# Overlapping the first two local-attention chunks, cutting TensorE work into shorter pieces, and a new set of plan constants, in a two-layer attention kernel

## The chip, the cores and the metric

One core of one Trainium2 chip runs the whole program. The metric is the device time of one execution in microseconds (us). The profile shows five engines, each with its own list of instructions: TensorE (PE in the profile; PEld is its weight loads), VectorE (DVE), ScalarE (ACT), GpSimd (POOL) and SyncE (SP).

## The reference, cut to what matters

```python
x = A_x                                                  # 1 x 2048 x 512, bf16
x = x + _A_ref(_layernorm(x), A_wqkv, A_wo)              # local attention
x = x + _B_ref(_layernorm(x), B_wq, B_wk, B_wv, B_wo)    # global attention
x = x + _A_ref(_layernorm(x), A_wqkv, A_wo)              # and both again,
x = x + _B_ref(_layernorm(x), B_wq, B_wk, B_wv, B_wo)    # with the same weights

# _A_ref: 32 heads of 16; position s sees s, s-2, ..., s-14 (8 keys, those below 0 masked)
# _B_ref: 32 query heads of 16, one shared key and value head, all 2048 keys, no mask
```

The global attention is the bulk: 32 heads x 2048 queries x 2048 keys, twice. The kernel cuts it into 4096 **tiles** of 128 keys x 512 queries. The local attention is done in **chunks** of 512 positions, four for each layer; a chunk's normalisation, projections, local attention and output come first, then the Q, K and V that the global attention of the layer needs from it.

## The kernel before: the parts that matter here

The kernel is a planner. While the program is built, each piece of work is an `Op` with the engines that may do it, the duration that the planner assumes, the pieces it depends on and a priority. The planner lays the pieces on the engines, and the order that comes out is the order in each engine's list. The stream of global tiles is a `Stream`, with biases in place of priorities. A smaller key goes first:

```python
MM, SWITCH, DMA = 216.0, 101.0, 620.0
...
class Sched:
    def cands(self, e):
        for op in self.open[e]:
            s = max(op.ready, self.free_at(op.want) if op.want else 0.0)
            ...
                yield (s + op.prio - 0.1 * (s - op.ready), s, op.ready, self.issue, (e, op))
        for src in self.sources:
            yield from src.cands(e)
...
class Stream:
    BIAS = {"act": 0.0, "act2": 150.0, "vec": 180.0, "pv": 200.0, "copy": 0.0, "pass": 140.0}
```

A global tile is a score matmul group and then an exponential. ScalarE takes two tiles at a time (`st` to `pt`); VectorE takes one (`dv`) through a 16-bit integer approximation, whose first pass on four tiles (`t` to `i`) also runs on VectorE and whose second runs on GpSimd. Then TensorE multiplies with V into `o`. So two engines share the exponentials, and the planner chooses which tile goes where.

A chunk's projections are pieces of four matmuls, its value matmuls pieces of 16:

```python
    def mm_full(self, pairs, deps, name, after=0.0):
        def emit(op):
            ps = self.psum(op, [128, 512], name=name)
            for n, (lhsT, rhs) in enumerate(pairs):
                self.chain("pe", self.nc.tensor.matmul(ps[:], lhsT=lhsT, rhs=rhs, start=(n == 0),
                                                       stop=(n == len(pairs) - 1)))
        return self.op("pe", len(pairs) * MM, emit, deps, want=("bank", "aux"), solid=True, prio=self.PRIO, after=after)

    def ln(self, src, deps, after=(0.0,) * 4, quick=False):
        ...                                              # statistics of four row tiles, on VectorE
            self.chain("dve", nc.vector.tensor_scalar_add(out=ve, in0=mv[:, :, 1], scalar1=EPS))
        ag = sm.used(self.op("dve", 560.0, aggr, st, prio=self.PRIO))
        pw = ...                                         # ve ** -0.5 on GpSimd
        nm = ...                                         # -mean * rstd on VectorE
```

A local **unit** is 128 of the 512 columns and half a chunk. It has two score groups; each gets its exponential (ScalarE), its mask (VectorE) and its multiplication with V and with ones for the denominators, together in one piece on TensorE. The tiles `q`, `k`, `v`, `xnT` and `oncA` of the local attention exist once, so a chunk's projections wait until the chunk before has let go of them.

Of the kernel before, what the change touches and what calls it, by code (L numbers as in the profile page):

```python
# [427 lines left out]
MM, SWITCH, DMA = 216.0, 101.0, 620.0  # L428
LAT = {"pe": 264.0, "act": 180.0, "dve": 142.0, "pool": 120.0, "sp": 2400.0}
POOL_COL = 1.75  # L430
FAR = float("inf")
# [10 lines left out]
class Op:  # L442

    def __init__(self, engs, emit, deps=(), want=None, frees=(), prio=0.0, mode="full", sub=0, then=None, after=0.0,
                 solid=False, port=()):
        self.engs, self.emit, self.deps, self.want, self.frees = engs, emit, list(deps), want, list(frees)
        self.prio, self.mode, self.sub, self.then, self.after = prio, mode, sub, then, after
        self.solid, self.port = solid, port
        self.end = self.eng = self.buf = None
        self.left, self.waiters = 0, []  # L450
# [5 lines left out]
class Sched:  # L456
# [12 lines left out]
    def add(self, op):  # L469
        op.left = 0  # L470
        for d in op.deps:
# [7 lines left out]
    def opened(self, op):  # L479
        op.ready = max([op.after] + [d.out() for d in op.deps])  # L480
# [31 lines left out]
    def pe_run(self, mode, sub, s, t=MM, solid=False):  # L512
# [4 lines left out]
        if solid:  # L517
            self.now["pe"] = max(s, s + t - MM) + 4
# [10 lines left out]
    def cands(self, e):  # L529
        for op in self.open[e]:  # L530
# [4 lines left out]
            if s < FAR:  # L535
                yield (s + op.prio - 0.1 * (s - op.ready), s, op.ready, self.issue, (e, op))
# [3 lines left out]
    def issue(self, s, what):  # L540
# [3 lines left out]
        if op.want:  # L544
            op.buf = self.take(op.want)
        t = op.engs[e]
# [7 lines left out]
        for h in op.frees:  # L554
            self.give(h.want, h.buf, op.out())
# [25 lines left out]
class Stream:  # L581

    GROUP = 4
    BIAS = {"act": 0.0, "act2": 150.0, "vec": 180.0, "pv": 200.0, "copy": 0.0, "pass": 140.0}
# [29 lines left out]

    def cands(self, e):
        S, B = self.s, self.BIAS
        if e == "pe":
            ok = self.next_ready()
            if ok < FAR:
                tl = self.tiles[self.pos]  # L620
                s = S.pe_start("row", tl[2], max(ok, S.free_at(("slot", "exp"))))
                if s < FAR:
                    yield (s + B["act2" if self.exps else "act"], s, 0.0, self.fill_slot, None)
                s = S.pe_start("row", tl[2], max(ok, S.free_at(("bank", "vec"))))
                if s < FAR:
                    yield (s + B["vec"], s, 0.0, self.fill_vec, None)
            if self.seg < len(self.segs):
                free = S.free_at(("bank", "o")) if self.bank is None else 0.0
                if free < FAR:
                    for n, (ok, tl, src) in enumerate(self.pvs[self.seg][:24]):  # L630
                        s = S.pe_start("col", tl[2], max(ok, free))
                        yield (s + B["pv"] + n * 0.01, s, 0.0, self.pv, n)
# [229 lines left out]

class Net:

    PRIO = 0.0

    def __init__(self, ctx, tc, w, S, nlayers, out_view):
# [33 lines left out]
        self.P = Ring([tile_(f"P{n}", [128, 2, UC], BF16) for n in range(4)])  # L901
# [5 lines left out]
        nc.gpsimd.memset(self.v.t[:, :, :, :, DH:2 * DH], 0.0)  # L907
# [6 lines left out]
        self.sched = Sched({"slot": 2, "bank": 4, **res}, {"bank": ((("vec", "aux"), 3), (("vec",), 2))})  # L914
        self.blocks = [(t, a) for t in range(4) for a in range(2)]
# [10 lines left out]
        self.xo, self.onb, self.ready, self.sums = {}, {}, {}, {}  # L926

# [59 lines left out]
    def mm_full(self, pairs, deps, name, after=0.0):  # L987

        def emit(op):
            ps = self.psum(op, [128, 512], name=name)  # L990
            for n, (lhsT, rhs) in enumerate(pairs):
                self.chain("pe", self.nc.tensor.matmul(ps[:], lhsT=lhsT, rhs=rhs, start=(n == 0),  # L992
                                                       stop=(n == len(pairs) - 1)))

        return self.op("pe", len(pairs) * MM, emit, deps, want=("bank", "aux"), solid=True, prio=self.PRIO, after=after)

    def ln(self, src, deps, after=(0.0,) * 4, quick=False):
# [5 lines left out]
        for i in range(4):  # L1003
# [3 lines left out]
            st.append(sm.used(self.op("dve", 596.0, emit, [*deps[i], *sm.prev], prio=self.PRIO, after=after[i])))  # L1007

        def aggr(op):
            for i in range(4):  # L1010
                self.chain("dve", nc.vector.bn_aggr(out=mv[:, i, :], in_=stats[:, i, :]))
            self.chain("dve", nc.vector.tensor_scalar_add(out=ve, in0=mv[:, :, 1], scalar1=EPS))

        ag = sm.used(self.op("dve", 560.0, aggr, st, prio=self.PRIO))
        pw = sm.used(self.op("pool", 1150.0, lambda op: self.chain("pool", nc.gpsimd.tensor_tensor(
            out=rstd, in0=ve, in1=self.w.nhalf[:], op=ALU.pow)), [ag], prio=self.PRIO))
# [640 lines left out]
```

## Time and profile before

| | before |
|---|---|
| median of 3 runs | 1650.68 us (1649.2 to 1652.32) |
| span of the profiled run | 1647.3 us |
| granted TensorE clock, mean | 0.933 |
| VectorE: work, idle | 1444.9, 202.4 us |
| ScalarE: work, idle | 1433.7, 213.6 us |
| tiles on ScalarE, on VectorE | 2618, 1478 |

Idle is the span less the busy time. The page of the kernel before gives the busy time of every engine, and for each group of instructions the count, the busy us, the mean ns of one, and the idle time of its engine just before it with what ended it:

```profile
PE 1542.2 (94%) x16661; PEld 522.3 (32%) x16661; DVE 1444.9 (88%) x2458; ACT 1433.7 (87%) x1751; POOL 906.0 (55%) x697
...
L1290 ACT ACTIVATE pt<-st 128x1024 bf16<-128x1024 f32 x1309 | 1223.0, 1091 | 87.9 <-PE st L1275 36.8
...
L1294 DVE TENSOR_SCALAR t<-dv 128x512 int16<-128x512 f32 x1478 | 926.4, 680 | 104.2 <-PE dv L1275 103.0
...
L1173 DVE TENSOR_TENSOR P<-P,bandmask 128x288 int32<-128x288 int32 x128 | 76.2, 632 | 7.1 <-ACT P L1167 6.2
```

TensorE is the busiest by this count, but its busy time holds waits within runs. What the second and third row say is plainer: the two engines that do the exponentials stood idle 87.9 and 104.2 us just in front of them. The waits of ScalarE say on whom (us in total, times, longest):

```profile
ACT pt L1290 <- PE st L1275: 36.8, 33, 3.7
ACT pt L1290 <- PE o L1315: 34.1, 21, 9.9
ACT xn L1026 <- DVE sm L1017: 20.8, 8, 10.6
ACT logs L1211 <- PE oa L1194: 19.6, 18, 3.9
...
ACT P L1167 <- PE st L1161: 11.6, 10, 2.8
```

All are TensorE, or the chain of the normalisation (`sm`): a score bank not yet filled (`st`), a buffer not yet multiplied away (`o`), a local unit's denominators not yet there (`logs`).

### The profile page before, as it was taken

The numbers are of one execution on the slowest core, as the hardware profiler recorded it, in microseconds if no ns is written. First come the engines' busy times: TensorE is split into PE (matmuls) and PEld (weight loads), VectorE is DVE, ScalarE is ACT, GpSimd is POOL, SyncE is SP. The second block draws the span as 40 slices with busy tenths as digits, with TensorE's granted clock in tenths as the row PEclk, the third lists the DMA queues.
The fourth block names the chain that finished last, engine by engine and source line by source line (L and its number), as shares of the span: only waits on it lengthen the run. The fifth ranks groups of instructions, "written<-read, shape, count | busy, mean of one in ns | idle before, by whom it ended". The sixth has DMA issues, their size and how long they took to land.

```text
span 1647.3 us, 41270 instructions
## 1 busy us (share of the span) xinstructions
PE 1542.2 (94%) x16661; PEld 522.3 (32%) x16661; DVE 1444.9 (88%) x2458; ACT 1433.7 (87%) x1751; POOL 906.0 (55%) x697
## 2 busy tenths in 40 slices
PE   5898999998999999999989999999999999999996
PEld 3443434322432234222332224322322222222221
DVE  5587777898699987999789996989999999999995
ACT  4677777896799978999889998899999999999993
POOL 5345443555456645566455654555666656665664
PEclk9879797999799997999989998899999999999998
DMA  4011111010110011000100001000100000000000
GB/s 130 15 15 26 15 27 16 14 35 22 25 16 13 12 21 25 18 12 18 31 11 22 12 12 27 15 4 16 42 12 12 12 25 15 12 12 28 15 12 15
DMA packets 92686, 34.45 MB, mean 21 GB/s; under 512 B 80264, under 2 KB 86024, under 8 KB 92488
## 3 DMA queue, kind: packets, MB, share of 16 engines
q1 hardware_dynamic: 91624, 29.91, 8.5%
q8 instruction: 132, 2.16, 0.5%
q10 hardware_dynamic: 864, 1.84, 0.3%
q14 instruction: 66, 0.54, 0.1%
HBM read 13.53 MB, written 2.61 MB: 10 GB/s over the span
## 4 chain that ended last, share of the span: by engine, by line
PE 42%; DVE 30%; ACT 17%; issue 8%; POOL 2%; DMA 0%; DVEq 0%; ACTq 0%; POOLq 0%
DVE t L1294 21%; ACT pt L1290 16%; PE o L1315 14%; PE st L1275 9%; PE dv L1275 3%; PE y L992 3%; DVE i L1303 3%; PE q L992 2%; PE k L992 2%; PE v L1112 2%; PE oa L1194 2%; PE oa L1186 2%; PE qb L992 2%; PE st L1161 1%; DVE P L1173 1%
## 5 line engine op out<-in xcount | busy, mean ns | idle before, releaser
L1290 ACT ACTIVATE pt<-st 128x1024 bf16<-128x1024 f32 x1309 | 1223.0, 1091 | 87.9 <-PE st L1275 36.8
L1299 POOL TENSOR_TENSOR i<-t,off 128x1024 int32<-128x1024 int32 x370 | 699.2, 1890 | 583.3 <-DVE i L1303 340.5
L1294 DVE TENSOR_SCALAR t<-dv 128x512 int16<-128x512 f32 x1478 | 926.4, 680 | 104.2 <-PE dv L1275 103.0
L1315 PE MATMUL o<-i,VEd 128*32 128x512 f16 x1472 | 275.8, 408 | 4.9 <-POOL i L1299 2.5
L1315 PE MATMUL o<-i,region 128*32 128x512 f16 x1484 | 273.2, 389 | 3.2 <-POOL i L1299 2.2
L1275 PE MATMUL st<-QT,KAB 32*128 32x512 bf16 x1312 | 259.1, 402 | 14.9 <-ACT pt L1290 12.1
L1275 PE MATMUL dv<-QT,KAB 32*128 32x512 bf16 x736 | 257.9, 400 | 11.3 <-DVE t L1294 10.1
L1303 DVE TENSOR_SCALAR i<-t 128x2048 int16<-128x2048 int16 x370 | 258.0, 698 | 8.3
L1275 PE MATMUL st<-QT,region 32*128 32x512 bf16 x1306 | 253.8, 386 | 11.8 <-ACT pt L1290 9.1
L1275 PE MATMUL dv<-QT,region 32*128 32x512 bf16 x742 | 256.0, 384 | 5.4 <-DVE t L1294 4.0
L1315 PE MATMUL o<-pt,region 128*32 128x512 bf16 x1306 | 254.2, 391 | 0.0
L1315 PE MATMUL o<-pt,VEa 128*32 128x512 bf16 x1312 | 250.3, 410 | 1.6 <-DVE X L1332 0.9
L1315 PE MATMUL o<-t,region 128*32 128x512 f16 x742 | 191.5, 390 | 0.6 <-DVE t L1294 0.6
L1315 PE MATMUL o<-t,VEd 128*32 128x512 f16 x736 | 189.2, 414 | 0.0
L1275 PEld LDWEIGHTS <-KAB 32*128 32x128 bf16 x2048 | 87.8, 92 | 261.3 <-issue 255.4
L1275 PEld LDWEIGHTS <-region 32*128 32x128 bf16 x2048 | 86.6, 91 | 256.3 <-issue 251.4
L1315 PEld LDWEIGHTS <-region 128*32 128x32 f16 (+1 forms) x3532 | 79.1, 94 | 191.3 <-issue 186.7
L1315 PEld LDWEIGHTS <-VEd 128*32 128x32 f16 x2208 | 77.7, 96 | 129.1 <-issue 121.2
L1167 ACT ACTIVATE P<-st 128x576 bf16<-128x576 f32 (+1 forms) x128 | 78.8, 652 | 12.7 <-PE st L1161 11.6
L1222 POOL TENSOR_TENSOR logs<-logs 128x256 f32<-128x256 f32 x64 | 43.3, 676 | 71.8 <-ACT rec L1213 71.7
L1173 DVE TENSOR_TENSOR P<-P,bandmask 128x288 int32<-128x288 int32 x128 | 76.2, 632 | 7.1 <-ACT P L1167 6.2
L1315 PEld LDWEIGHTS <-VEa 128*32 128x32 bf16 x1312 | 57.7, 96 | 74.7 <-issue 70.6
(136 smaller groups left out, 1166.0 us busy)
## 6 DMA issues: line engine op xcount, KB each, us to landing
lb<-rd SPq DMA_DIRECT2D x31, 256.0 KB
X<-X SPq DMA_DIRECT2D x124, 32.0 KB
k<-oncA SPq DMA_DIRECT2D x56, 64.0 KB
w_sb<-in_A_wqkv_dram ACTq DMA_DIRECT2D x4, 384.0 KB
region<-in_A_x_dram SPq DMA_DIRECT2D x3, 512.0 KB
out_dram<-w_sb SPq DMA_DIRECT2D x3, 512.0 KB
S<-X SPq DMA_DIRECT2D x62, 8.0 KB
rd<-R SPq DMA_DIRECT2D x62, 8.0 KB
```

Of the source, the lines that this page charges most:

```text
L992: self.chain("pe", self.nc.tensor.matmul(ps[:], lhsT=lhsT, rhs=rhs, start=(n == 0), stop=(n == len(pairs) - 1)))
L1112: self.chain("pe", nc.tensor.matmul(ps[64 * a:64 * a + 64, i], lhsT=self.xnT.t[:, kt, kb * 64:(kb + 1) * 64], rhs=wv[:, kt, a, :, :], star ...
L1167: ex = self.op("act", act_ns(2 * ncol), lambda op, P=P, sc=sc: self.chain("act", nc.scalar.activation(out=P.t[:, :, c0:UC], in_=self.st.po ...
L1173: self.chain(op.eng, self.pick(op).tensor_tensor(out=x, in0=x, in1=self.w.band[:].unsqueeze(1).to_broadcast([128, 8, NQ // 2]), op=ALU.bit ...
L1186: self.chain("pe", nc.tensor.matmul(o[32 * r:32 * r + 32, 0, q0:q0 + w], lhsT=vv[64 * a:64 * a + 64, j, 16 * gh:16 * gh + 32], rhs=P.t[64 ...
L1222: self.chain("pool", nc.gpsimd.tensor_tensor(out=lg.t[:], in0=lg.t[:], in1=lg.t[:], op=ALU.mult))
L1275: self.chain("pe", self.nc.tensor.matmul(out, lhsT=self.KAB[l][32 * g:32 * g + 32, a, kt * 128:(kt + 1) * 128], rhs=self.QT[32 * g:32 * g ...
L1290: self.chain("act", self.nc.scalar.activation(out=self.pt[pt][:, 0:n, :], in_=self.st.pop(key)[:, 0:n, :], func=AF.Exp, scale=E_SCALE))
L1294: self.chain("dve", self.nc.vector.tensor_scalar(out=self.t[buf][:, r, :].bitcast(I16), in0=self.dv[bank][:], scalar1=-U_BIAS, scalar2=U_B ...
L1299: i = self.nc.gpsimd.tensor_tensor(out=self.i[out][:, 0:n, :].bitcast(I32), in0=self.t[buf][:, 0:n, :].bitcast(I32), in1=self.w.off2[:, 0: ...
L1303: i = self.nc.vector.tensor_scalar(out=self.i[out][:, 0:n, :].bitcast(I16), in0=self.t[buf][:, 0:n, :].bitcast(I16), scalar1=J_OFF[j], sca ...
L1315: self.chain("pe", self.nc.tensor.matmul(self.o[bank][32 * g:32 * g + 32, :], lhsT=lhsT, rhs=rhs, start=first, stop=last, tile_position=(0 ...
```

## The change

Four edits of structure and a new set of constants came together:

1. **Overlap.** The first layer's second chunk gets its own set of tiles, lent from places that are not used yet (an unused half of QT, four X accumulators, `lb`, part of KAB, one pass buffer). It no longer waits for the first chunk's.
2. **Shorter pieces.** A projection is two pieces of two matmuls, a value piece is eight matmuls, and a unit's multiplication with V is two pieces, its denominators a third. The planner may put a tile between them.
3. **Masks and normalisation.** One mask of 576 columns in place of two of 288; the add and the multiplication of the normalisation's scalars move from VectorE to GpSimd.
4. **Constants.** Every priority has a new value, so have the biases; two new rules hold back TensorE work that would delay a due tile, and let PV matmuls gather. The durations that the planner assumes changed too (a local score group 170 ns, before 300), and so did the moment from which it plans on after such a TensorE piece.

```diff
-MM, SWITCH, DMA = 216.0, 101.0, 620.0
+MM, SWITCH, DMA = 216.0, 96.0, 620.0
+AGE = 0.054
+SLACK, PATIENCE = 575.3, 176.5
...
+        due = min((src.due() for src in self.sources), default=FAR) if e == "pe" else FAR
...
-                yield (s + op.prio - 0.1 * (s - op.ready), s, op.ready, self.issue, (e, op))
+                key = s + op.prio - AGE * (s - op.ready)
+                if s + op.engs[e] + SWITCH > due + SLACK and s - op.ready < PATIENCE:
+                    key = max(key, due + 1.0)
+                yield (key, s, op.ready, self.issue, (e, op))
...
-    BIAS = {"act": 0.0, "act2": 150.0, "vec": 180.0, "pv": 200.0, "copy": 0.0, "pass": 140.0}
+    BIAS = {"act": -17.5, "act2": 659.7, "vec": 264.7, "pv": 140.5, "pv_in": 210.7, "batch": 14, "few": 9.7,
+            "copy": 15.3, "pass": 430.3}
...
-        return self.op("pe", len(pairs) * MM, emit, deps, want=("bank", "aux"), solid=True, prio=self.PRIO, after=after)
+        a = self.op("pe", half * MM, emit, deps, want=("bank", "aux"), solid=True, prio=410.8 + self.PRIO)
+        b = self.op("pe", half * MM, rest, behind=[a], solid=True, prio=-2800.5 + self.PRIO)
+        b.want, b.lend = None, a
+        return b
...
-        ag = sm.used(self.op("dve", 560.0, aggr, st, prio=self.PRIO))
-        pw = ...        # power on GpSimd
-        nm = ...        # multiplication on VectorE
+        ag = sm.used(self.op("dve", 280.0, aggr, st, prio=-922.7 + self.PRIO))
+        nm = sm.used(self.op("pool", 1700.0, scalars, [ag], prio=447.4 + self.PRIO))
...
-        n = ... {"act": 830.0, "dve": 690.0, "pool": 940.0} ... prio=self.PRIO
+        n = ... {"act": 830.0, "dve": 690.0, "pool": 940.0} ... prio=194.2 + self.PRIO
...
+        B = self.sets[int(first and c == 1)]
+        quick = first and c < 2
...
-            ms = self.op("dve", 500.0, mask, [ex], prio=self.PRIO, port=("dve",))       # twice a unit
+        ms = P.used(self.op("dve", 800.0, mask, exps, prio=-656.0 + self.PRIO, port=("dve",)))
...
-            m = self.op("pe", 340.0 + SWITCH + 150.0, pv, ...)                           # twice a unit
+        p0 = self.op("pe", 165.0, lambda op: pv(op, 0), ..., prio=48.8 + self.PRIO, want=("bank", "aux"))
+        p1 = self.op("pe", 165.0, lambda op: pv(op, 1), behind=[p0], ..., prio=-272.8 + self.PRIO)
+        m = self.op("pe", 300.0, dn, behind=[p1], solid=True, mode="h64", prio=-458.3 + self.PRIO)
```

## The prediction

> **What bounds the kernel now.** I read the page first: its busy shares (TensorE 94%, VectorE 88%, ScalarE 87%) name no single bound, so I cut the span into stages at the places where the projections of a chunk stand, and read the busy table of those stages.
>
> ```profile
> PEclk9879797999799997999989998899999999999998
> ...
> 0.00:65.00 65.00, 40.69 (x676) 23.81 (x676) 38.63 (x83) 31.82 (x59) 32.60 (x76) 0.89 0.30 83
> 65.00:150.00 85.00, 79.92 (x1040) 34.05 (x1036) 66.18 (x118) 65.51 (x97) 39.63 (x33) 0.84 0.12 20
> ...
> 584.00:681.00 97.00, 92.75 (x1161) 37.37 (x1160) 77.34 (x135) 80.39 (x110) 45.78 (x38) 0.86 0.14 23
> 681.00:785.00 104.00, 101.69 (x959) 26.33 (x956) 100.60 (x168) 102.18 (x113) 62.89 (x40) 0.97 0.05 14
> ...
> 1075.00:1610.00 535.00, 520.22 (x4872) 146.16 (x4866) 526.54 (x871) 521.66 (x567) 332.23 (x206) 0.99 0.06 16
> ```
>
> The first line is the granted clock in 40 slices of the span, in tenths. In the others, columns after the stage's length: busy us of TensorE, its weight loads, VectorE, ScalarE, GpSimd, then the granted clock. There are two kinds of stage. Without local-attention work (681 to 785, 1075 to 1610) VectorE and ScalarE are both 97 to 98% busy at clock 0.97 to 0.99: they share the exponentials of the global attention and neither has room. With a local-attention chunk (65 to 150, 584 to 681) both fall to about 80%, TensorE stays at 94 to 96%, and the clock is 0.84 to 0.86. Summed over VectorE and ScalarE, idle time is 60 us in the first 65 us, 273 us in the seven later chunk stages (32 to 46 each), 41 us in the tail after 1610, and about 42 us in all the rest. The chunk stages are where a change can earn anything.
>
> Why they idle is in the timeline of one such stage:
>
> ```profile
> 412.66 1.03 PE L992 MATMUL q<-xnT,w_sb 128*128 128x512 bf16 x4
> ...
> 413.53 1.03 PE L992 MATMUL k<-xnT,w_sb 128*128 128x512 bf16 x4
> ...
> 414.48 3.68 PE L1112 MATMUL v<-w_sb,xnT 128*64 128x256 bf16 x64
> ...
> 418.81 1.29 DVE L1294 TENSOR_SCALAR t<-dv 128x512 int16<-128x512 f32 x2 [9.36 <-PE dv L1275]
> ```
>
> Eight projections and then 64 value matmuls stand back to back, 10.5 us without one score matmul; VectorE waited 9.36 us for its next score tile. The waits view says the same of the whole run: 103 us of VectorE idle behind the score bank (dv). So in chunk stages TensorE's order starves the other two.
>
> Counting score tiles in the trace gives the scale. Between tile 2642 (1181.4 us) and tile 3672 (1490.1 us) one of the 4096 tiles takes 0.300 us. The second chunk's stage (64.9 to 149.9 us) completes 128 tiles: 38 us of tiles, 47 us extra. The later chunks cost 43 to 51 us extra each. With the first chunk (no tile before 64.9 us) that is some 390 us beyond 4096 x 0.300 = 1228 us.
>
> **What the Trainium skill says.** "TensorE: Matmul & The Clock Gate", Part 1, says that the granted clock is either half or full, set by how busy the array has been. The trace agrees: in ten-us windows it reads 0.50 at 180 to 190, 260 to 270 and 430 to 440, where the small local-attention matmuls stand close together, and 1.00 in the plain stages. The same page, "Back-to-back issue gap", gives about 216 ns for 512 columns at full clock; the q and k groups here start 0.86 us apart for four, 0.215 each. "SBUF — State Buffer", "SBUF: two separate sides", says that VectorE and GpSimd share a port pair under an exclusive lock, also for a VectorE instruction with two SBUF inputs against a GpSimd one. The trace agrees strikingly:
>
> ```profile
> L1012 DVE TENSOR_SCALAR sm<-sm x16: 170/172/4655, 8.6 to 1056.7; 128x4 f32<-128x4 f32 x16
> ...
> L1017 DVE SCALAR_TENSOR_TENSOR sm<-sm x16: 156/1506/1852, 14.4 to 1058.6; 128x4 f32<-128x4 f32 x16
> ```
>
> Minimum, median and maximum in ns: a two-input instruction on four columns needs 156 ns and takes 1506 ns at the median, with GpSimd in its 1.9 us passes beside it.
>
> **The change, part by part.** I built the changed program and counted its instructions by engine, and took each duration from a row of the trace before.
>
> LN scalars on GpSimd: L1012 and L1017 leave VectorE. Busy 15.6 + 12.1 us, less one 4.7 us outlier in the prologue: 23 us off VectorE, and one hop fewer per normalisation.
>
> Masks: 128 of 288 columns (76.2 us busy, 595 ns each, floor 387) become 64 of 576. Twice the floor less some overhead plus one lock wait, estimated 0.9 us: 57 us, so 19 us off VectorE.
>
> New plan: VectorE's tiles fall from 1478 to 1428 (50 x 0.627 = 31 us) and its first passes from 370 to 358 (12 x 0.698 = 8 us); ScalarE gets 25 more exponentials of two tiles (25 x 0.934 = 23 us). Evacuations move a little: about 9 us onto VectorE, and about 12 us off ScalarE, mostly normalisations of x that now run on GpSimd. VectorE's work goes from 1445 to about 1373 us, ScalarE's from 1434 to about 1445 us.
>
> Shorter pieces: projections in halves, value matmuls in eights, PV and denominators apart. I added up TensorE's work along both orders (0.216 us per four score or PV matmuls, 0.107 per change of array mode, from the 0.323 us at which three scores give way to PV) and took the stretches between two scores for one consumer. What exceeds 2 us falls from 123 to 88 us for ScalarE's tiles and from 148 to 141 us for VectorE's. At clock 0.86 that is 40 and 9 us less starvation. The 10 us block survives: six gaps above 6 us remain of eight, and q, k, v still follow each other in the third to eighth chunk. Local units stand as close together as before (34 tiles among them in one chunk, 40 before), so I expect the same clock dips.
>
> First two chunks overlapped: the second gets its own tiles and a TensorE transpose, so its q projection follows the first chunk's Q at once instead of at 72.8 us, and the wait between its v (83.4 us) and its scores (88.8 us), for the DMA that splits k, goes. It is through at tile 100, not 128. This is partly in the sums above; alone I put it at 13 us.
>
> The sum, seen from each engine: ScalarE 1445 + idle 213.6 - 40 = 1619 us; VectorE 1373 + idle 202.4 - 9 = 1566 us. Both must hold for one span, and tiles can move between them, so I take the middle, 1592, plus 3 us between span and run time: 1596. Part of VectorE's saved work lies in stages where it starves anyway and buys nothing there, so I choose 1602.
>
> **The rivals.** First, TensorE takes over as the bound: mode changes rise from 2716 to 2782 and, because PV runs are shorter, its summed work from about 1257 to 1276 us. Chunk stages are already 94 to 96% busy there. Against it: busy time contains waits inside runs, and the sum is only 76% of the span. If it holds, the gain shrinks to the second chunk's and some of the starvation: 1630 to 1640. Second, VectorE starvation is what counts and is hardly touched (148 to 141): the saved VectorE work becomes idle time and ScalarE sets the time, about 1620. Third, the plan's many new constants fit the chip better than my count shows, and chunk stages shrink towards the ideal: the local work of ScalarE (211 us) and VectorE (about 160 us) shared evenly is some 23 us per chunk against 46; a third of that difference over seven chunks is 54 us, and with the work saved about 1570. Fourth, borrowed tiles make something wait (X, lb, one pass buffer of four): their owners are needed only after tile 64, so I expect nothing.
>
> **Range and chances.** The first rival gives the top, the third the bottom: 1568 to 1637 us. The 2% line is 1617.7; only the first two rivals lie above it. Faster 0.70, same 0.28, slower 0.02, as nothing found lengthens the span as a whole.
>
> **What would show it.** VectorE busy near 1373 and ScalarE near 1445; the first chunk-stage pair through by about 130 us at tile 100; plain stages unchanged at 0.300 us per tile; later chunk stages shorter by 3 to 6 us of extra each, with the 9 us VectorE wait behind q, k, v still there; clock near 0.93. It is wrong if plain stages slow down, if GpSimd's longer LN chain delays projections, or if chunk stages change by more than 10 us each.

## The result, and the profile after

| | before | after |
|---|---|---|
| median | 1649.94 us (1642.1 to 1652.32, 4 runs) | 1586.88 us (1580.98 to 1590.64, 4 runs) |
| ratio | | 0.9622, 95% interval 0.9574 to 0.9671 |
| span of the profiled run | 1647.3 us | 1588.9 us |
| granted clock, mean | 0.933 | 0.957 |
| VectorE: work, idle | 1444.9, 202.4 us | 1387.2, 201.7 us |
| ScalarE: work, idle | 1433.7, 213.6 us | 1441.6, 147.3 us |

A ratio here is the mean time of one kernel's fast runs over that of the other's of the same rounds, so it is not quite the ratio of the medians. The changed kernel is faster by 3.8%, some 63 us. The page after:

```profile
PE 1499.4 (94%) x16593; PEld 502.9 (32%) x16593; DVE 1387.2 (87%) x2320; ACT 1441.6 (91%) x1755; POOL 918.6 (58%) x751
...
PEclk9888799999899999999979998999998999999998
...
L1379 ACT ACTIVATE pt<-st 128x1024 bf16<-128x1024 f32 x1334 | 1248.9, 1082 | 53.1 <-PE dv L1364 21.4
...
L1383 DVE TENSOR_SCALAR t<-dv 128x512 int16<-128x512 f32 x1428 | 896.3, 681 | 30.6 <-PE dv L1364 29.9
...
L1252 ACT ACTIVATE P<-st 128x576 bf16<-128x576 f32 (+1 forms) x128 | 82.5, 665 | 1.6 <-PE st L1245 1.4
...
L1259 DVE TENSOR_TENSOR P<-P,bandmask 128x576 int32<-128x576 int32 x64 | 59.1, 926 | 15.5 <-ACT P L1252 13.3
```

VectorE's work is down 58 us and ScalarE's up 8. ScalarE's idle time is down 66 us, VectorE's as good as unchanged. The PEclk line has fewer 7s than that in the prediction. The waits of ScalarE after:

```profile
ACT pt L1379 <- PE dv L1364: 21.4, 32, 2.9
ACT xn L1089 <- POOL sm L1078: 18.3, 2, 12.3
ACT pt L1379 <- PE st L1364: 15.0, 34, 1.1
ACT pt L1379 <- PE o L1404: 14.0, 20, 4.1
...
ACT logs L1300 <- PE oa L1284: 9.7, 15, 1.8
```

The waits for `st` and `o` fell from 36.8 and 34.1 to 15.0 and 14.0 us, that for the denominators from 19.6 to 9.7, and that of the local exponential (`P`) from 11.6 to 1.4. Two did not fall: what is put down to `dv` rose from 14.9 to 21.4, and the normalisation's scalars, which now come from GpSimd, are still waited for 18.3 us (20.8 before), in two waits in place of eight. VectorE's waits after:

```profile
DVE v L1021 <- PE v L1196: 48.8, 7, 12.4
DVE oncA L1306 <- ACT rec L1302: 31.8, 25, 4.1
DVE t L1383 <- PE dv L1364: 29.9, 33, 3.1
```

Here one wait took the place of another. Before, VectorE waited 103.0 us for score tiles. Now it waits 29.9 for these, and 48.8 in seven waits of up to 12.4 us for the value matmuls `v`: VectorE has no tile to work on before that either; only another piece comes next in its list. The two sum to some 24 us less than the 103.0; what rose in return are the waits for ScalarE's reciprocals (20.8 to 31.8 us) and for its local exponentials (6.2 to 13.3). The timeline of the fifth chunk shows the wait for `v`:

```profile
401.68 1.02 PE L1045 MATMUL k<-xnT,w_sb 128*128 128x512 bf16 x4
...
406.86 1.03 PE L1045 MATMUL k<-xnT,w_sb 128*128 128x512 bf16 x4
...
407.81 3.68 PE L1196 MATMUL v<-w_sb,xnT 128*64 128x256 bf16 x64
...
410.23 0.69 DVE L1021 CAST v<-v 128x512 bf16<-128x512 f32 x1 [7.42 <-PE v L1196]
...
411.44 0.39 PE L1364 MATMUL dv<-QT,KAB 32*128 32x512 bf16 x2
```

From 401.68 to 411.4 us TensorE runs projections and value matmuls back to back, and no score. VectorE has been idle for 7.42 us when the first V comes. This is the same 10 us block as before the change.

The busy time of the first two stages and of the pair from 560.8 to 746.8 us (columns as in the prediction: length, then busy us of TensorE, weight loads, VectorE, ScalarE, GpSimd, then clock):

```profile
0.00:66.60 66.60, 39.93 (x692) 24.82 (x693) 37.54 (x69) 32.88 (x65) 35.73 (x93) 0.90 0.28 81
66.60:137.80 71.20, 67.67 (x937) 28.88 (x936) 48.43 (x88) 59.82 (x90) 32.89 (x34) 0.83 0.05 9
...
560.80:666.30 105.50, 101.55 (x1338) 39.83 (x1335) 90.67 (x156) 97.76 (x130) 63.21 (x56) 0.98 0.13 25
666.30:746.80 80.50, 79.16 (x760) 20.85 (x759) 78.75 (x130) 79.78 (x88) 49.89 (x31) 1.00 0.05 12
```

The chunk stage of the second layer from 560.8 to 666.3 now has ScalarE busy 93%, VectorE 86%, at clock 0.98; before it was 83%, 80%, 0.86. It is the best of its kind: the other three of the second layer have ScalarE at 90%, VectorE at 80 to 82% and a clock of 0.92 to 0.94. Counting tiles gives the same as one number for each stage. The table has the **extra** of a stage: its length less 0.300 us for each global tile that was issued in it. The first starts with the first global tile, and a stage ends where the last Q projection of its chunk starts.

| stage ends with chunk | 2 | 3 | 4 | 5 | 6 | 7 | 8 | tail |
|---|---|---|---|---|---|---|---|---|
| before, us | 45.9 | 46.9 | 44.4 | 52.0 | 45.1 | 42.7 | 46.4 | 30.1 |
| after, us | 40.3 | 42.6 | 35.0 | 39.6 | 32.7 | 38.3 | 36.4 | 27.8 |

The seven stages sum to 323.4 and 264.9 us. The difference of 58.5 is the whole gain: the first tile comes 2.6 us later (67.6 us after 65.0), the tail is 2.3 shorter, and 58.5 - 2.6 + 2.3 = 58.2, with 58.4 between the spans. The question for the experiments is which part of the change does this.

### The profile page after: what moved, and what is told of

Same layout as the page of the kernel before. It is cut to its first block, busy times and chain, and to the rows that moved or that the text cites. A ratio compares the mean times of both kernels' runs of the same rounds, so it can differ in the third digit from the quotient of the medians.

```text
span 1588.9 us, 40977 instructions
## 1 busy us (share of the span) xinstructions
PE 1499.4 (94%) x16593; PEld 502.9 (32%) x16593; DVE 1387.2 (87%) x2320; ACT 1441.6 (91%) x1755; POOL 918.6 (58%) x751
## 4 chain that ended last, share of the span: by engine, by line
PE 43%; DVE 26%; ACT 19%; issue 8%; SPq 1%; DMA 1%; POOL 1%; ACTq 0%; DVEq 0%; POOLq 0%
DVE t L1383 20%; PE o L1404 16%; ACT pt L1379 16%; PE st L1364 11%; PE dv L1364 2%; PE y L1045 2%; DVE i L1392 2%; PE q L1045 2%; ACT P L1252 2%; PE k L1045 2%; PE qb L1045 2%; SPq L1177 1%; PE oa L1284 1%; PE oa L1272 1%; PE st L1245 1%
## 5 line engine op out<-in xcount | busy, mean ns | idle before, releaser
L1379 ACT ACTIVATE pt<-st 128x1024 bf16<-128x1024 f32 x1334 | 1248.9, 1082 | 53.1 <-PE dv L1364 21.4
L1388 POOL TENSOR_TENSOR i<-t,off 128x1024 int32<-128x1024 int32 (+1 forms) x358 | 676.1, 1889 | 527.4 <-DVE i L1392 331.6
L1383 DVE TENSOR_SCALAR t<-dv 128x512 int16<-128x512 f32 x1428 | 896.3, 681 | 30.6 <-PE dv L1364 29.9
L1364 PE MATMUL st<-QT,KAB 32*128 32x512 bf16 x1348 | 269.9, 394 | 13.1 <-ACT pt L1379 10.4
L1364 PE MATMUL st<-QT,region 32*128 32x512 bf16 x1320 | 259.7, 386 | 6.5 <-ACT pt L1379 4.7
L1404 PE MATMUL o<-i,VEd 128*32 128x512 f16 x1400 | 261.8, 398 | 0.7 <-DVE i L1392 0.2
L1404 PE MATMUL o<-pt,VEa 128*32 128x512 bf16 x1348 | 259.7, 402 | 0.8 <-DVE t L1383 0.5
L1392 DVE TENSOR_SCALAR i<-t 128x2048 int16<-128x2048 int16 (+1 forms) x358 | 251.2, 702 | 10.2
L1364 PE MATMUL dv<-QT,KAB 32*128 32x512 bf16 x700 | 239.9, 389 | 4.5 <-DVE t L1383 2.8
L1259 DVE TENSOR_TENSOR P<-P,bandmask 128x576 int32<-128x576 int32 x64 | 59.1, 926 | 15.5 <-ACT P L1252 13.3
```

The source lines that it names most:

```text
L1259: self.chain("dve", nc.vector.tensor_tensor(out=x, in0=x, in1=self.w.band[:].unsqueeze(1).to_broadcast([128, 16, NQ // 2]), op=ALU.bitwise ...
L1364: self.chain("pe", self.nc.tensor.matmul(out, lhsT=self.KAB[l][32 * g:32 * g + 32, a, kt * 128:(kt + 1) * 128], rhs=self.QT[32 * g:32 * g ...
L1379: self.chain("act", self.nc.scalar.activation(out=self.pt[pt][:, 0:n, :], in_=self.st.pop(key)[:, 0:n, :], func=AF.Exp, scale=E_SCALE))
L1383: self.chain("dve", self.nc.vector.tensor_scalar(out=self.t[buf][:, r, :].bitcast(I16), in0=self.dv[bank][:], scalar1=-U_BIAS, scalar2=U_B ...
L1388: i = self.nc.gpsimd.tensor_tensor(out=self.i[out][:, 0:n, :].bitcast(I32), in0=self.t[buf][:, 0:n, :].bitcast(I32), in1=self.w.off2[:, 0: ...
L1392: i = self.nc.vector.tensor_scalar(out=self.i[out][:, 0:n, :].bitcast(I16), in0=self.t[buf][:, 0:n, :].bitcast(I16), scalar1=J_OFF[j], sca ...
```

## The experiments

Twelve kernels were run, each four times. All start from the kernel after and set something back, but for the control. Times are medians; the kernel before had medians of 1648.6 to 1650.7 us in these rounds. Losses are against the median of the kernel after, 1586.88 us, which was not run again beside them. The intervals of the ratios are some 5 us to each side, so losses of 12 to 18 us can't be ranked among themselves. All outputs are right.

### How large is chance?

The new plan is one of many that such constants give, and a lucky one would look like a gain. The control changes one constant that is only the planner's guess of a mode change:

```diff
-MM, SWITCH, DMA = 216.0, 96.0, 620.0
+MM, SWITCH, DMA = 216.0, 98.0, 620.0
```

> A control: the changed kernel with the planner's assumed cost of a mode change at 98 ns in place of 96. Same instructions in kind, another order. It tells how far any edit moves the time through a reshuffled plan alone. Both theories: within 8 us of the changed kernel, 1579 to 1595 us. If it is over 1600, the changed kernel's order is a lucky one and differences of the other runs under 15 us mean nothing.

**1586.18 us**, ratio 0.9621 (0.9594 to 0.9648). The plan changes (VectorE has 1427 tiles, not 1428, and the order differs) and the time doesn't. So the plan after is not a single lucky order. But this is one small reshuffle; how far larger ones would move the time, no run measures.

### Constants or structure?

Two runs take the halves apart. In the first the structure of the kernel after runs with every constant as before (and the two new rules off):

```diff
-AGE = 0.054
-SLACK, PATIENCE = 575.3, 176.5
+AGE = 0.1
+SLACK, PATIENCE = FAR, 0.0
-    BIAS = {"act": -17.5, "act2": 659.7, ...}
+    BIAS = {"act": 0.0, "act2": 150.0, "vec": 180.0, "pv": 200.0, "pv_in": 200.0, "batch": 0, "few": 0.0,
+            "copy": 0.0, "pass": 140.0}
-        a = self.op("pe", half * MM, emit, ..., prio=410.8 + self.PRIO)
+        a = self.op("pe", half * MM, emit, ..., prio=self.PRIO)
...      # and so on for every priority
```

> The changed kernel with every constant of the plan as before (all priorities, biases, aging, no hold-back rule for pieces that would delay a due score, no batching of PV), its structure (borrowed tiles, pieces, LN scalars, one mask per unit) kept. If the structure brings the gain: 1590 to 1605 us. If the new order from the constants brings it: 1630 to 1650, with ScalarE idle back near 200 us (147 in the changed kernel, 214 before).

**1652.54 us**, ratio 1.0038 (1.0000 to 1.0075): the structure alone gains nothing. Its ScalarE waits for `o` and `st` are much like those of the kernel before:

```profile
ACT pt L1379 <- PE o L1404: 35.3, 28, 4.2
ACT pt L1379 <- PE st L1364: 30.0, 37, 3.3
...
ACT logs L1300 <- PE oa L1284: 14.2, 15, 3.8
```

In the second, the new constants run with the structure undone: no overlap, whole projections and value pieces, PV with denominators, two masks, normalisation scalars on VectorE (the edits of the next part, together). It is not quite the old structure: a unit's multiplications with V are one piece here and were two before, each with its own denominators.

```diff
-        self.sets = [self.own_set(), self.lent_set()]
+        self.sets = [self.own_set()] * 2
-        a = ... ; b = ...                        # a projection in two pieces
+        return self.op("pe", len(pairs) * MM, emit, ..., prio=410.8 + self.PRIO)
-        ms = P.used(self.op("dve", 800.0, mask, exps, ...))
+        ms, ms1 = [P.used(self.op("dve", 450.0, ..., [exps[gh]], ...)) for gh in range(2)]
...      # and the edits of the next part
```

> The changed kernel with its constants kept and its structure undone: own tiles for the second chunk, LN scalars on VectorE, projections, value matmuls and PV with denominators as whole pieces, a mask for each half. If the structure brings the gain: 1630 to 1650 us. If the constants do: 1595 to 1610.

**1622.31 us**, ratio 0.9827 (0.9793 to 0.9861): the constants alone gain 27 us, between the two results that were expected. Nothing and 27 make 63 together. The parts are not additive: the remaining 36 us need both. The new assumed durations are in both runs, so what these do alone stays open. Where structure and constants need each other in the first layer, the next experiment shows.

### The parts of the structure, one undone at a time

**The overlap undone.** The second chunk uses the first one's tiles again, its normalised x goes through the DMA transpose, and its k through the DMA that splits it. The run doesn't tell the tiles from the DMAs.

```diff
-        self.sets = [self.own_set(), self.lent_set()]
+        self.sets = [self.own_set()] * 2
-        quick = first and c < 2
+        quick = first and c == 0
-        if first and c == 1:
-            self.lend(B, adds)
...      # and nothing is lent: no pass buffer held back, no waits on what was borrowed
```

> The changed kernel with the second chunk in the first chunk's own tiles again, with the DMA that splits k and the DMA transposes; everything else as changed. If the borrowed tiles are worth what the prediction gave them (13 us), the time is 1600 us. If they are the main part of the gain, as the change's name suggests, 1620 to 1630. If only what the stage table shows is theirs (the second chunk's stage lost 5 us of extra time and the first gained 2), 1588 to 1592.

**1613.84 us**, ratio 0.9785 (0.9742 to 0.9827): undoing the overlap costs 27 us, twice what was predicted for it. The stages of the second, third and fourth chunk, whose extra is 52.8, 43.7 and 49.7 us here, carry the loss (28.3 us against the kernel after); the four of the second layer are within 2 us of it.

```profile
64.60:156.00 91.40, 75.64 (x1037) 31.99 (x1040) 61.80 (x107) 66.25 (x97) 39.31 (x37) 0.83 0.11 19
156.00:238.00 82.00, 71.27 (x986) 30.79 (x988) 58.60 (x97) 66.52 (x97) 37.41 (x35) 0.94 0.13 21
238.00:326.00 88.00, 78.90 (x1034) 32.82 (x1036) 57.80 (x96) 64.00 (x95) 36.35 (x38) 0.84 0.11 20
```

Both engines are at 66 to 81% in these three. The reason is in the count of tiles. A first-layer chunk gives 128 tiles to the stream; no more can be issued before the next chunk's Q and K are there. The time between the last tile of such a supply and the next tile, from the trace, in us:

| | at tile 128 | at 256 | at 384 |
|---|---|---|---|
| before | 8.8 | 0.0 | 0.9 |
| after | 0.0 | 0.0 | 4.6 |
| overlap undone | 23.3 | 15.8 | 16.1 |
| new constants without the structure | 13.0 | 14.9 | 8.2 |
| structure with the old constants | 0.0 | 5.8 | 0.9 |

With the new constants the stream runs ahead of the chunk work. In the first layer this ends with the stream using up its supply, and both engines have no tile until the late chunk comes. The overlap brings the second chunk forward (its Q is done at tile 100), and the supply lasts. This is one place where structure and constants need each other. It is less than half of what the constants alone lack: their kernel has 14.7 us more extra than the kernel after in the stages of chunks 2 to 4, and 21.9 us more in the four of the second layer, where no run shows why. Nor is a us without a tile a us lost: here 50.6 us more of it go with 28.3 us of extra, and the kernel with old priorities of the local units, told of below, has 23.4 us of it and loses 12.

**The normalisation's scalars back on VectorE.**

```diff
-        nm = sm.used(self.op("pool", 1700.0, scalars, [ag], prio=447.4 + self.PRIO))
+        pw = sm.used(self.op("pool", 1150.0, scalars, [ag], prio=447.4 + self.PRIO))     # the power only
+        nm = sm.used(self.op("dve", 250.0, ..., [pw], prio=self.PRIO))                   # -mean * rstd
```

> The changed kernel with the LN scalars back on VectorE (add of eps and the two-input product there, the power alone on GpSimd), all else as changed. VectorE gets some 23 us of busy time back, its two-input instruction waiting about 1.5 us each for GpSimd. If VectorE's fixed work counts in full: 1598 us (half of 23 us). If VectorE starves in those stages anyway, as its unchanged idle time of 202 us suggests: 1584 to 1592.

**1600.95 us**, ratio 0.9708 (0.9668 to 0.9747): 14 us. That is near the half of 23 us that was expected, but not quite as expected: the two rows take 20.8 us here, 5.5 of them one outlier at the start; the two-input instruction takes 167 ns at the median and not 1506, and 12.7 us in all (15.6 before); and VectorE's busy time is up 11 us in all.

**Whole projections and value pieces.**

```diff
-        a = self.op("pe", half * MM, emit, ..., prio=410.8 + self.PRIO)
-        b = self.op("pe", half * MM, rest, behind=[a], solid=True, prio=-2800.5 + self.PRIO)
+        return self.op("pe", len(pairs) * MM, emit, ..., prio=410.8 + self.PRIO)
...      # the value matmuls likewise: one piece of 900 ns with prio 612.4
```

> The changed kernel with each projection and each group of 16 value matmuls as one piece again; PV, denominators, masks and constants as changed. If shorter pieces are what lets scores in between: 1605 us or more and ScalarE's idle time up from 147 by 20 us. Since the order of the changed kernel puts no score between most halves: 1583 to 1593, no effect.

**1599.63 us**, ratio 0.9688 (0.9657 to 0.9719): 13 us, between the two results that were expected (ScalarE's idle time is up 8 us, not 20). VectorE's wait for score tiles is back, as one line of its waits shows:

```profile
DVE t L1368 <- PE dv L1349: 89.9, 43, 12.7
```

89.9 us, with a longest of 12.7. But the sum of VectorE's idle time is only 11 us above that of the kernel after (213.0 against 201.7): mostly the wait has changed its name again, from `v` to `t`. A wait that vanishes from a list must be looked for under other names before it is counted as a gain.

**PV and denominators of a unit in one piece** (before the change they were two, one for each score group).

```diff
-        p0 = self.op("pe", 165.0, lambda op: pv(op, 0), ...)
-        p1 = self.op("pe", 165.0, lambda op: pv(op, 1), behind=[p0], ...)
-        m = self.op("pe", 300.0, dn, behind=[p1], solid=True, mode="h64", prio=-458.3 + self.PRIO)
+        p0 = m = self.op("pe", 630.0, lambda op: (pv(op, 0), pv(op, 1), dn(op)), ...,
+                         mode="c64", prio=48.8 + self.PRIO, want=("bank", "aux"))
```

> The changed kernel with PV of both halves and the denominators of a unit as one piece, all else as changed. If the shorter pieces matter here as they did for projections (e6 cost 13 us): 1595 to 1605. If not: 1580 to 1592, since the order of the changed kernel already puts nothing between them in almost all units.

**1604.99 us**, ratio 0.9714 (0.9683 to 0.9745): 18 us.

The four single losses sum to 72 us (27 + 14 + 13 + 18), yet all of the structure undone together, the masks too, costs 35 (1622.31 against 1586.88). What one part is worth depends on the others being there, and the whole pieces keep only the first half's priority. None of these figures is a part's own worth.

### The parts of the constants

**The stream's biases as before.**

```diff
-    BIAS = {"act": -17.5, "act2": 659.7, "vec": 264.7, "pv": 140.5, "pv_in": 210.7, "batch": 14, "few": 9.7,
-            "copy": 15.3, "pass": 430.3}
+    BIAS = {"act": 0.0, "act2": 150.0, "vec": 180.0, "pv": 200.0, "pv_in": 200.0, "batch": 0, "few": 0.0,
+            "copy": 0.0, "pass": 140.0}
```

> The changed kernel with only the biases of the stream as before: second exponential slot 150 for 660, VectorE's scores 180 for 265, PV 200 flat with no waiting for a batch of 14, first pass 140 for 430. The old constants together cost 66 us. If the stream's biases carry it: 1625 or more. If the priorities of the chunks' own pieces do: 1595 to 1605.

**1602.88 us**, ratio 0.9714 (0.9676 to 0.9753): 16 us.

**All priorities of pieces as before**, biases and the new rules kept.

```diff
-        a = ... prio=410.8 + self.PRIO)
+        a = ... prio=self.PRIO)
-        m = self.op("pe", 300.0, dn, behind=[p1], solid=True, mode="h64", prio=-458.3 + self.PRIO)
+        m = self.op("pe", 300.0, dn, behind=[p1], solid=True, mode="h64", prio=self.PRIO - 100.0)
...      # every prio=, and the second chunk's 35.5
```

> The complement: the changed kernel's stream biases, aging and hold-back rule kept, the priorities of all chunk pieces (projections +411 and -2801, values +612, unit scores -228, masks -656, PV +49 to -458 and so on) back to before's zeros, -50 and -100. If the priorities carry the gain: 1625 or more. If the stream's biases do: 1595 to 1605.

**1643.87 us**, ratio 0.9973 (0.9937 to 1.0009): 57 us, so nearly the whole gain hangs on the priorities. Three runs split them into groups. First those of the projections and value pieces alone:

```diff
-        a = ... prio=410.8 + self.PRIO)
-        b = ... prio=-2800.5 + self.PRIO)
+        a = ... prio=self.PRIO)
+        b = ... prio=self.PRIO)
-            m0 = ... prio=612.4 + self.PRIO)
-            m = ... prio=-32.3 + self.PRIO)
+            m0 = ... prio=self.PRIO)
+            m = ... prio=self.PRIO)
```

> Of the piece priorities, whose loss together cost 57 us, only the four of the projections and value matmuls go back to zero (first half +411, second half -2801, first value piece +612, second -32). If what counts is that projections are held back until the stream has its scores: 1620 to 1640 us, the chunks of the second half complete at a lower tile number (near 760 as before, 845 in the changed kernel) and the later chunk stages are back at 42 us of extra each. If the units' or the LN priorities count: 1590 to 1600.

**1600.54 us**, ratio 0.9704 (0.9679 to 0.9729): 14 us. The theory that holding back the projections is what counts asked for 1620 to 1640 and fell, although the fifth chunk is through at tile 767, as it said. In the profiled run the whole loss lies at the start: all of the second chunk's projections and value matmuls now come before the first global tile.

```profile
75.24 3.68 PE L1196 MATMUL v<-w_sb,QT 128*64 128x256 bf16 x64
...
78.85 0.39 PE L1364 MATMUL st<-QT,KAB 32*128 32x512 bf16 x2
```

The first tile comes at 78.9 us and not at 67.6, while the seven stages sum to 261.4 us of extra, less than the 264.9 of the kernel after. Then those of a local unit's pieces (scores, exponentials, mask, PV, denominators, reciprocals):

```diff
-        ms = ... prio=-656.0 + self.PRIO, port=("dve",)))
+        ms = ... prio=self.PRIO, port=("dve",)))
-        m = ... prio=-458.3 + self.PRIO)
+        m = ... prio=self.PRIO - 100.0)
...      # and the seven others of a unit
```

> The complement: the nine priorities of the local-attention units (scores, exponentials, masks, PV, denominators, their logs and products) back to before's, those of the projections kept as changed. If the projections' hold-back is what counts: 1590 to 1602 us. If the units' order is: 1615 to 1640.

**1598.94 us**, ratio 0.9673 (0.9644 to 0.9702): 12 us. By its expectation this speaks for the projections, against which the previous run spoke; so neither group alone carries the gain. And last all the others: normalisations, transposes, evacuations, additions and what closes a block.

```diff
-        ag = sm.used(self.op("dve", 280.0, aggr, st, prio=-922.7 + self.PRIO))
-        nm = sm.used(self.op("pool", 1700.0, scalars, [ag], prio=447.4 + self.PRIO))
+        ag = sm.used(self.op("dve", 280.0, aggr, st, prio=self.PRIO))
+        nm = sm.used(self.op("pool", 1700.0, scalars, [ag], prio=self.PRIO))
-        n = ... prio=194.2 + self.PRIO, port=("pool",))))
+        n = ... prio=self.PRIO, port=("pool",))))
...      # 16 more, and the second chunk's 35.5
```

> The kernel after with the new priorities kept for the projections, the value matmuls and the pieces of a local unit, and the old ones for everything else (the normalisations and their scalars, transposes, evacuations and additions of output, the work that closes a block), and no extra lateness for the second chunk. Setting all priorities back cost 57 us, those of the projections alone 14 and those of the units alone 12. Theory one, the rest carry the gain: about 30 us lost, 1610 to 1625. Theory two, the groups stand in for one another and the large loss comes only when all go: 5 to 15 us lost, 1592 to 1602, as with each of the other two groups alone. Theory three, projections and units together carry it: within 5 us of the kernel after.

**1614.71 us**, ratio 0.9794 (0.9761 to 0.9827): 28 us. The three groups lose 14 + 12 + 28 = 54 us one by one, and 57 together. Among the priorities, then, the parts add up within the intervals, and half of their gain is in pieces that look like side work.

What these do can be read from the groups of instructions. Which engine scales a row tile of x (`xn`) is the planner's choice; the kernel after, ScalarE and GpSimd:

```profile
L1089 ACT ACTIVATE xn<-x_sb,sm 128x512 bf16<-128x512 f32 x7 | 5.8, 863 | 6.0 <-POOL sm L1078 6.0
```

```profile
L1092 POOL TENSOR_SCALAR xn<-x_sb,sm 128x512 bf16<-128x512 f32 x21 | 22.3, 1067 | 0.4
```

and with the old priorities of the last group:

```profile
L1089 ACT ACTIVATE xn<-x_sb,sm 128x512 bf16<-128x512 f32 x20 | 15.6, 830 | 6.9 <-POOL sm L1078 6.8
```

```profile
L1092 POOL TENSOR_SCALAR xn<-x_sb,sm 128x512 bf16<-128x512 f32 x6 | 6.2, 1038 | 0.6
```

Thirteen more of these run on ScalarE, which has no room, and 15 fewer on GpSimd, which is 58% busy. ScalarE then does 9 fewer pairs of tiles (1325 against 1334) and VectorE 18 more (1446 against 1428). Counting the tiles of x that come from the first layer too, the kernels before, with old constants, with all old priorities and with this last group have 21 to 25 of 64 on ScalarE, the kernel after and the control 9 and 8. The trace shows the shift; that the old priority of `xn` alone makes it, no run separates, and with the new one the kernel without overlap has 19 too.

### One ledger for all

For every run, span = (work + idle) / 2, when work and idle are summed over ScalarE and VectorE, because each engine's busy and idle time fill the span. Only these two terms can change the span. This is bookkeeping, true of any two engines: it says where the time lies and not what caused it. It holds for the profiled run alone, which may lie at either end of its four: the scalars on VectorE cost 14 us in the median and 6.4 in these spans. From the pages:

| kernel | median | span | work | idle |
|---|---|---|---|---|
| before | 1649.94 | 1647.3 | 2878.6 | 416.0 |
| structure, old constants | 1652.54 | 1648.5 | 2860.2 | 436.8 |
| all priorities old | 1643.87 | 1632.1 | 2856.0 | 408.2 |
| constants, old structure | 1622.31 | 1622.0 | 2855.1 | 388.9 |
| other priorities old | 1614.71 | 1611.1 | 2858.1 | 364.1 |
| overlap undone | 1613.84 | 1611.4 | 2827.9 | 394.9 |
| PV whole | 1604.99 | 1603.9 | 2844.0 | 363.8 |
| biases old | 1602.88 | 1598.0 | 2825.5 | 370.5 |
| scalars on VectorE | 1600.95 | 1595.3 | 2839.7 | 350.9 |
| projection priorities old | 1600.54 | 1596.9 | 2836.4 | 357.4 |
| projections whole | 1599.63 | 1601.1 | 2833.7 | 368.5 |
| unit priorities old | 1598.94 | 1599.4 | 2837.2 | 361.6 |
| after | 1586.88 | 1588.9 | 2828.8 | 349.0 |
| control | 1586.18 | 1584.5 | 2829.9 | 339.1 |

Of the gain of 58.4 us in the span, half of 49.8 is less work and half of 67.0 is less idle time: 25 and 33 us. The overlap works through idle time alone (395 against 349). The priorities of the last group work mostly through work (29 us of it, 15 of idle time): of the 29, the rows show 11.6 us of copies and 6.8 of first passes on VectorE, 11.5 us more of `xn` on ScalarE and 5.9 on VectorE, less 6.2 for the nine pairs.

**The clock** is a rival. Its mean rose from 0.933 to 0.957. The records of the trace show it at one half or at full, so time at half clock is 2 x (1 - clock) x span: 221 us in the profiled run before, 137 after. What it costs can be read between runs of one kernel, where the order is fixed and the clock still differs. Of the four runs of the kernel after, 149 us of it go with a span of 1588.5 us and 111 with 1579.2. The 28 runs of the kernel before have 200 to 234 us of it and 1639.2 to 1650.9 us of span. Over all 80 runs of the fourteen kernels, each set against the mean of its own kernel, the span grows by 0.31 us for each us more at half clock (standard error 0.015; single kernels 0.24 to 0.39, but for the control and the last group of priorities).

At that rate, as an estimate, the 84 us less would be 26 of the 58 us between the spans, so nearly half of the gain may come by way of the clock. It isn't shown that the rate holds from one order to another: the kernel with old projection priorities has the highest clock of all (0.974) and runs 14 us longer than the kernel after. And no run sets the clock and leaves the order, so whatever raised the clock is itself part of the change. The single losses move as well at that rate: whole projections have 36 us more at half clock in the mean of the four runs, 11 of their 13 us.

## Why the prediction was right, and where its sizes were off

- **The bound: right.** The seven chunk stages carry all of the gain (58.5 us), and the tiles of the last long plain stage took 0.302 us, not more than 1% from 0.300.
- **VectorE's work: right in its parts, 14 us short in the sum.** Copies fell by 30.1 us (predicted 31), first passes by 6.8 (8), masks by 17.1 (19; 926 ns each, predicted 0.9 us), the two scalar rows by 27.7 with their outlier (23 without), evacuations rose by 9.4 (9). Other rows rose by some 6 us, and the sum of rows fell by 67 us, where the busy time fell by 58, since it counts overlap of neighbours once. So VectorE has 1387 us, not 1373. ScalarE's 1441.6 against 1445 was right.
- **The LN scalars: right in size.** 23 us of VectorE's work are about half as much of span, and setting them back costs 14. The two-input instruction's 1.5 us at the median did not come back with them (167 ns).
- **Starvation: the main size that was off.** The prediction counted stretches without a score for each engine along the new order and got 40 us for ScalarE and 9 for VectorE. The profile shows 66 and 1. The direction was right for both. What the count can't see are waits for other things than a score: the buffers that PV frees (34.1 to 14.0 us), the denominators (19.6 to 9.7), the local exponentials' scores. These are over 40 us of ScalarE's 66.
- **The 10 us block: right.** It survives, and VectorE now waits in it for `v`. "Later chunk stages shorter by 3 to 6 us of extra each" was too little: chunks 4 to 8 gave 9.4, 12.4, 12.4, 4.4 and 10.0 us. So one of its own signs of being wrong, a chunk stage that changes by more than 10 us, came true in two stages.
- **The overlap: right in kind, half the size.** Chunk 2 is through at tile 100, but at 137.8 us and not by 130. It was put at 13 us for the wait it removes in the kernel before. In the kernel after, its use is larger: it keeps the stream supplied at tiles 128, 256 and 384, where undoing it leaves 55 us without a tile. Undoing it costs 27 us.
- **The clock: wrong.** "The same clock dips" and 0.93 did not come; it is 0.957. The sum had no term for it, and by the estimate above it may be 26 us of span, so part of the idle time that the prediction put down to order may be the clock's.
- **The last step: wrong.** The balance of both engines gave 1592 us of span, and 1588.9 was measured, with work 11 us above and idle time 18 below what was put in. Then 3 us were added for the gap between span and run (measured 1.7) and 6 because part of VectorE's saving would "buy nothing". The measured sum leaves no room for such a loss. So 1602 lay 15 us above 1586.88, within the range. That the balance came so near is partly luck: its work was too small, its idle time too large, and the two errors cancel to 3 us.
- **The rivals.** TensorE as the new bound asked for 1630 to 1640 us and fell by the time. That it limits the chunk stages now is not excluded: it is busy 95.6 to 97.1% in the four of the second layer (92.8 to 95.6% before), waits within runs included. (The prediction's "94 to 96%" and clock "0.84 to 0.86" for chunk stages are those of the two it shows; the seven have 91 to 96% and 0.84 to 0.92.) "VectorE starvation is what counts" fell: its idle time is unchanged, and the time still went down. The borrowed tiles made nothing wait that the profile shows. The third rival, that the constants fit better than the count shows, was closest with its 1570: without them the whole structure gains nothing. But no rival said that structure and constants need each other.

What stays open: how much of the gain comes by way of the clock, what the planner's new assumed durations do, where structure and constants need each other in the second layer, which of the 20 constants in the last group does its work, and the pure worth of the merged masks, which no run undid alone. No variant beat the kernel after by more than its own spread.

## What to carry to other kernels

Where a planner or a list of priorities decides the order, an edit of the structure can gain nothing under constants made for the old one, as here (0 us alone, 63 with new ones): run the edit with the old constants and the constants without the edit before crediting either. Sum work and idle time over the engines that share the bound; the half-sum for two engines is the span, and it shows whether a part saves work, saves waiting, or only renames a wait. Set the runs of one kernel against each other before judging the clock: with the order fixed they give its price. And look where side work lands that more than one engine can do: the priorities of such pieces were worth 28 us here, those of the projections and the units 14 and 12.

## What the Trainium skill lacked or had wrong

- "TensorE: Matmul & The Clock Gate", Terms, puts the loss to a throttled clock at the throttled time times (1 - K/N), here half of it. Between runs of one kernel the span here grew by 0.31 us for each us more at half clock (80 runs of fourteen kernels), so for this kernel the figure is too high.
- "Perfetto Trace Analysis", Optimizing Scalar/DVE Operations, says that moving operations between VectorE and GpSimd might not help, as they share a port. Here it did: 32 instructions on four columns took 27.7 us on VectorE, the 48 that replace them take 13.0 us on GpSimd, and setting them back cost 14 us. The two-input ones took 156 ns at least and 975 on average on VectorE in the kernel before.
- The same section advises to break up ScalarE's and VectorE's instructions when they aren't saturated and make bubbles on other engines. It doesn't say so of TensorE's work, where shorter runs of unchanged instructions paid here: 13 us for projections in halves, 18 us for PV and denominators apart, with the new constants.
- No page says that a change of structure and the order's constants must be judged together: 0 us, 27 us, and 63 us for both.
